# Local attention beside a long convolution on one core: projections and turning in row halves, other engines for taps, filter sums and gate, a new order

## The chip, the cores and the metric

The kernel runs on one core of a Trainium2 chip. The metric is the device time of one execution in microseconds (us). A second execution, taken with the hardware profiler, gives the profile: what each engine did and when. The core has a matrix engine (TensorE, PE in the profile; its weight loads are shown apart as PEld), VectorE (DVE), ScalarE (ACT), GpSimd (POOL), SyncE (SP, which here only starts transfers), and DMA queues. TensorE sums into PSUM, a memory of eight banks; everything else lies in the on-chip memory SBUF.

## The reference

Two independent parts, whose results stand side by side in the output (2048 rows of 1152 columns, bf16). Part A is attention over a short, dilated window; part B is a shift convolution of four taps, a product, a convolution as long as the sequence, and two more products.

```python
# part A: x is 2048 x 576, 32 heads of 18
qkv = x @ wqkv                                  # wqkv is 576 x 1728
idx = pos[:, None] - 2 * arange(8)[None, :]     # each row sees itself and 7 earlier rows, every second one
logits = einsum("bhsd,bhswd->bhsw", q, k[idx]) * 18 ** -0.5      # idx < 0: -1e9
o = einsum("bhsw,bhswd->bhsd", softmax(logits), v[idx])
a = o.reshape(1, 2048, 576) @ wo
# part B: q, k, v are 2048 x 576
kv = (sum of k shifted by t = 0..3 rows, times shift_k[:, 3 - t]) * v
y = irfft(rfft(kv, 4096) * rfft(ssm_k, 4096))[:2048] + kv * ssm_D
b = q * y
return concatenate([a, b], axis=-1)
```

## The kernel before, in words

**Storage and order.** All data lie in one SBUF tile, `mem`, at offsets worked out by hand; so nearly every row of the profile reads `mem`. PSUM is the tile `PS`: eight banks, used as four pairs. The work is a list of 675 named steps (`Op`; 745 after the change). A step may take one or two pairs of PSUM banks (a `Box`), hold them over several steps, and give them back. The string `ORDER`, a table of numbers in base 36, sets in which order the steps are emitted; a number divided by six is the step, and the remainder says which pair it takes, or, for a step that takes none and can go to either engine (`move`), that VectorE does it (remainder 1) and not ScalarE. Each engine and each DMA queue then does its own instructions in that order, and waits on semaphores for the others. So a step that waits holds up everything behind it on its engine.

**Start.** L330 (`heat`) runs 13 matmuls on zeros. `load_w` brings the projection weights, 576 columns of each of q, k and v (`comp` 0, 1, 2) in one transfer for the first four row blocks of 128 and two copies of the last 64 rows. x comes transposed by DMA (L196), except rows 512 to 1023, which come as they are and are turned on TensorE (`turn_x`, L316).

**Projections** (`project`). A unit computes one column tile `ct` (five of them: four of 128, one of 64) of one `comp` for one half `hh` of the sequence (1024 rows). The contraction runs over four row blocks of 128 (`full`, L419, matmuls on the whole array) and one of 64 (`tails`, L429: two matmuls, each on one half of the array's rows, working at the same time). The v units and the last column tile also split the array's columns in two. ScalarE copies the result out (L445; L450 for the last tile). For v, GpSimd then copies 16 edge columns between the blocks (`edges`, L402), and short DMAs do so for the last tile (`p14`, `p24`).

**Attention.** Logits: VectorE multiplies q with four shifted k at once (`l`, L473), TensorE sums the products over a head with 0/1 matrices (`L`, L481). After softmax, VectorE multiplies the weights with shifted v (`w`, L725), TensorE sums over the window (`a`, L739, two PSUM pairs), ScalarE copies the sums out (L745), and TensorE multiplies by `wo` (L790, whose result ScalarE copies out, L795).

**Convolution.** Per pair of row blocks, `taps` runs the four shifted products as diagonal matmuls into PSUM (L535), in two halves, one with its rows backwards. VectorE multiplies the result in PSUM by v (L543). `fold` turns the product: it forms a sum and a difference of the two halves while it transposes, as two matmuls of 256 columns with the joined matrices identity and plus or minus identity (`F1`, `F2`; L556, L557, and L570, L571 for the last columns). ScalarE copies the result (L561, L575). The filter gets the same treatment once (`load_filter`, `fold_filter`): a copy `ho` of its upper half is negated (`hn`), and ten accumulating DMAs from GpSimd's queue add the lower half. Then come the spectra of the filter (L581, L582, L605, L606) and of the input (L645, L660), each copied out by `move` (L188 on VectorE, L190 on ScalarE); their products on VectorE (L835, `products`), summed on TensorE (L859) and copied out (L870); the way back by L892 and L896; and the `gate`: VectorE forms the upper half and multiplies it by q (L911, L912), TensorE mirrors the lower half with the matrices that `flip` builds on GpSimd (L921), and VectorE multiplies that, out of PSUM, by q (L925).

Of the kernel before, what the change touches and what calls it, by code (L numbers as in the profile page):

```python
# [17 lines left out]
1o u 26 0 10 20 6 86 8u 1c 90 c 1u 7c 8c 6o 6u 2p 70 2c 96 2u 32 19 36 2i 1i 76 b0 66 3o bx 3u 3c 3i  # L18
a8 80 5c cp c0 40 b6 i c6 130 o 1ki ac ar ai 5i bc 4o cu 6i au 4i bi no dl bo o0 5o d0 dw nv e0 d6
oo 5u ce dc e6 oc 4c o6 ci ou 8i 46 oi po 9c i0 fk do 8o el 7i 7o fo p0 7u ew eo 1f6 136 pc rc 14c  # L20
f9 f0 4u pi fc 9w qc p6 a0 9l pu q0 9o qi i8 50 qo hl 140 qu 14v ho q6 150 ic r0 56 ii 13p r6 60 14l
13e 156 13u ri j6 ro 14o k7 13i jc 16o 146 jq ji kc ir 18c ki ju m1 hu fu k0 6c m6 mc iu 16c 15c j0
177 xo g0 kr 17u 17c l0 15i ku lp y0 l6 16x n6 xw 170 186 g6 lu yc 180 16i 161 18u gl ru ec 166 s0
17i gc s6 y6 go yi yo mi 15p lf 15u gv li z0 17o 1al 19u yu 1ao z6 zc h0 h9 sc 1fv 190 mu zo hc 1a9
1g0 zi zu 1ac 100 1g6 1hd 18i n0 19i tx 1hi 10c 19c 106 1ho 1j1 1hu 10u 1a0 mo 18o u0 110 u6 10i 196
116 si uf 19o so 1ji ui uo su t0 1i3 1jo 10o t6 tc 1i6 11c 1ik 11i ti to 1mc 1k3 1io 11o 1mi 11u uu
1iu 120 1gw v0 1mo v6 1mu 1bu 126 1fc nc 1h0 12c 12i 1j6 12o 1h6 1bk 1k6 wj 12u 1l0 1bo 1lo vx wo
1ku 1ge 1n6 1lu 1fi 1q6 w0 1fo ni 240 1n0 1gi 1oi 23f 1ou 246 w7 1go 1p0 23i wu 1oo 1nc wc vf x0 1d1
26e vi 1d6 vo 1ju 1dc 1ni 26i 1ic 1av 1di 1dq 1b0 233 1o0 1jc 2f0 1m0 1no 236 1ko 1du 1li 1qi 24e
1pc 1nu 1qc 263 1qo 24i 1cc 1pi 251 266 1e2 256 1o9 1e6 1p6 26p 1ci 25e 26u 1c0 1oc 1b7 1po 25i 25r  # L30
1c6 23q 1bc 1qu 1su 25u 1pu 1l6 23u 1lc 1so 2k0 1cq 1q0 24r 1ec 1r6 1m6 1si x6 1z1 1kc xc xi 1sc 1r0
1zi 1z6 1cu 201 1zo 1rc 1zu 1eu 1zc 20k 1f0 206 1ru 24u 1ri 20o 1ro 1t0 20u 1s2 1uf 1ui 1u0 1t6 1ej
1s6 1vo 1wl 1u6 1ww 1wo 280 1y6 1x0 27f 1tc 1eo 1w8 211 1wc 27i 1ti 27q 216 223 286 2fi 1to 27u 226
2fo 22c 1vx 1tu 20c 1ye 2fu 21c 2fc 1w0 2go 2g0 1yi 1xx 2g6 21k 1y1 2hi 2gu 21o 22l 2h0 21u 2ju 1ve
22o 2m0 2ho 1vj 1ur 22u 2hu 2k6 2ko 28e 1uu 28o 2nc 1yp 28i 1x9 1yu 28v 272 1xc 2li 2kc 276 2ki 1v3
2ku 2ge 1v6 2pu 2l0 2lo 2lu 2gi 2h9 2qc 2m6 292 2hc 2mc 29o 296 2ad 2mu 1xl 2ai 2i2 2f6 1xo 2l7 2wc
2i6 29u 2n2 2po 2qu 2n6 2mi 2ni 2q0 2mo 2j8 2no 2ic 2b3 2lc 2jc 2q6 2ro 2b6 2qi 2qo 2bc 2bl 2r0 2s0
2si 29e 2r6 2oo 29i 2cj 2ii 2bo 2ou 2nw 2co 2tc 2cu 2ru 2o0 2bu 2s6 2to 2sc 2u6 2aq 2so 2e3 2au 2su
2p0 2o6 2d1 2p6 2oc 2iw 2e6 2a0 2wu 2d6 2c3 2a6 2dc 2ti 2c6 2tu 2u0 2j0 2cc 2rf 2uc 2wi 2ji 2ek 2ri
2xc 2ui 2wo 2t3 2eo 2eu 2zi 2x0 2io 2t6 2x6 2pc 2xi 2xo 2oi 2vl 2xu 2dk 300 2zc 2do 2zo 2zu 326 306  # L40
30c 2jo 2uq 30i 32o 2uu 30o 2pi 2du 321 30u 2ec 32c 2v0 32i 32u 2vo 330 2vu 336 2v6 2y3 310 2vc 2w0
31j 2y6 33e 316 2w6 31o 2yc 31u 2yv 2yi 33i 31c 2z0 2yo 348 33o 2z6 33u 34c 340 34i
# [7 lines left out]
PAIRS = ((0, 1), (1, 2), (2, 3))  # L50


class Box:


    ps, step = None, 1024


class Op:
# [3 lines left out]
    vector = False  # L63
# [5 lines left out]
def emit(op, slot, PS):  # L69
    if op.take:  # L70
        a, b = (slot, slot + 1) if op.take == 1 else PAIRS[slot]
        op.box.ps, op.box.step = PS[:, 2 * a:2 * a + 2], 1024 * (b - a)
    Op.vector = slot == 1 and not op.take
    op.fn()
# [10 lines left out]
def kernel(  # L85
# [13 lines left out]
    nc = tc.nc  # L99
# [206 lines left out]
    def turn_x():  # L306

        dma("xn", M(OT1, [[D, 4], [1, D]]), xf[512:1024, :].rearrange("(sb p) c -> p sb c", p=128), nc.scalar)
        for u in range(3):
# [3 lines left out]
            def unit(box=box, kbs=kbs):  # L313
# [7 lines left out]
            op(f"nx{u}e", (lambda box=box, dst=dst: act(dst, box.ps, ACT.Copy)) if u < 2 else  # L321
               (lambda box=box, dst=dst: nc.vector.tensor_copy(dst, box.ps[:, 0:1, :])), box, free=True)
# [80 lines left out]

    def project(comp, ct, hh):
        o, pad = ((qat, 0), (kat, PAD), (vat, PAD))[comp]
        o = o(ct, hh)
        box = Box()
        nm = f"p{comp}{ct}{hh}"
        cols = (0,) if comp < 2 and ct < 4 else (0, 1)
        jps = (0, 1) if ct < 4 else (0,)  # L410
        tail_first = (comp == 1) if comp < 2 else ct % 2 == 1
        two = comp == 0 and hh == 0 and ct < 4

        def full(jp, first, last):
            for kb in range(4):
                ws = wcol(comp, kb, ct)
                for a in cols:
                    p = slice(64 * a, 64 * a + 64) if len(cols) > 1 else slice(0, 128)
                    mm(box.ps[p, jp, :], ws[a % len(ws)], xT(kb, 1024 * hh + 512 * (jp ^ a), 512),  # L419
# [585 lines left out]
```

## Time and profile before

| | |
|---|---|
| timed runs | 209.07, 209.44, 209.53 us (median 209.44) |
| the profiled execution's span | 207.9 us |
| time around that span, against the median | 1.54 us |
| instructions in it | 7147 |
| PE, matmuls | 3173 |
| DVE / ACT / POOL instructions | 147 / 173 / 105 |

The span is what the profiler records from the first instruction to the last. Below, "busy" is the share of the span in which an engine had an instruction running; a slice is a fortieth of the span, some 5.2 us, and its digit the busy share in tenths. A row with a time in front is from the timeline: start and length in us of a run of like instructions, engine, line, tile, and the form of the operands (`xN` counts them). A row that starts with a line number is a group of like instructions over the whole span: busy time, mean length of one in ns, and behind the second bar the engine's idle time just ahead of them and what ended it. A row from the view of waits has the engine, the waiting line, what released it, and then the sum, the number and the longest of these waits. On TensorE, matmuls of one kind overlap in the records (one of 512 columns lasts 0.39 us there, though the next starts long before), so the distance from start to start is the cost, not the length of one.

### The profile page before, as it was taken

The page shows a single profiled execution, that of the slowest core. Times are in us where ns is not written, and L with a number is a line of the kernel's source. Part 1 is how long each engine was busy: PE and PEld are TensorE (multiplying, and loading weights), DVE is VectorE, ACT ScalarE, POOL GpSimd, SP SyncE. Part 2 cuts the span into 40 slices and gives each one's busy share as a digit, 9 for nine tenths or more (in the row PEclk, how much of TensorE's full clock was granted, in tenths as well). Part 3 has the DMA queues.
Part 4 walks back from the last instruction along what each step waited for, and adds up shares of the span by engine and source line. Part 5 has one row for each costly group of instructions (what it writes and reads, how often), then busy time and mean ns, then how long its engine had stood idle before and what let it go on. Part 6 is the DMA issues. An engine that isn't in the chain of part 4 may idle for free.

```text
span 207.9 us, 7147 instructions
## 1 busy us (share of the span) xinstructions
PE 197.1 (95%) x3173; PEld 133.1 (64%) x3173; DVE 177.1 (85%) x147; ACT 142.3 (68%) x173; POOL 56.9 (27%) x105
## 2 busy tenths in 40 slices
PE   7899999999999999999998969998999999999991
PEld 2433334554644557778787857685689878787690
DVE  7306899769878898889999998999999998999963
ACT  2525479875977715578989857988898767665541
POOL 7981033001041195010899900000003020110000
PEclk9999999999999999999999999999999999999998
DMA  6998979999999959945880263106345865749834
GB/s 170 225 223 150 199 150 194 162 185 130 116 180 213 203 99 188 184 110 120 181 221 6 42 162 103 32 3 199 126 167 114 230 177 141 184 131 255 260 126 114
DMA packets 55254, 32.09 MB, mean 154 GB/s; under 512 B 42032, under 2 KB 52408, under 8 KB 55224
## 3 DMA queue, kind: packets, MB, share of 16 engines
q1 hardware_dynamic: 52520, 26.33, 57.2%
q0 software_dynamic: 2176, 4.73, 13.3%
q10 hardware_dynamic: 528, 0.59, 1.0%
q8 instruction: 24, 0.39, 0.8%
q14 instruction: 6, 0.05, 0.1%
HBM read 5.90 MB, written 4.72 MB: 51 GB/s over the span
## 4 chain that ended last, share of the span: by engine, by line
PE 84%; DMA 5%; ACT 5%; DVE 2%; SPq 1%; issue 1%; DVEq 0%
PE PS L419 24%; PE PS L790 10%; PE PS L892 7%; PE PS L859 6%; PE PS L660 5%; PE PS L481 5%; PE PS L429 4%; PE PS L535 4%; PE PS L645 3%; PE PS L739 3%; ACT mem L745 3%; DMA mem<-in_A_wqkv_dram 3%; DMA mem<-in_A_wo_dram 2%; PE PS L581 2%; PE PS L921 2%; DVE mem L725 2%
## 5 line engine op out<-in xcount | busy, mean ns | idle before, releaser
L419 PE MATMUL PS<-mem 128*64 128x512 bf16 (+1 forms) x304 | 51.5, 385 | 0.7 <-DMA mem<-in_A_wqkv_dram 0.7
L473 DVE TENSOR_TENSOR mem<-mem 128x4096 bf16<-128x4096 bf16 (+1 forms) x20 | 40.7, 2074 | 7.0 <-PE PS L481 4.2
L725 DVE TENSOR_TENSOR mem<-mem 128x4096 bf16<-128x4096 bf16 x18 | 40.3, 2290 | 1.9 <-PE PS L739 1.2
L419 PEld LDWEIGHTS <-mem 128*64 128x64 bf16 (+1 forms) x304 | 26.6, 144 | 22.1 <-issue 6.8
L835 DVE TENSOR_TENSOR mem<-mem 128x4608 bf16<-128x4608 bf16 (+3 forms) x21 | 38.4, 1867 | 1.6 <-PE PS L859 1.4
L190 ACT ACTIVATE mem<-PS 128x768 bf16<-128x768 f32 (+1 forms) x49 | 35.2, 761 | 5.8 <-PE PS L582 2.7
L445 ACT ACTIVATE mem<-PS 128x1024 bf16<-128x1024 f32 x24 | 24.2, 1022 | 19.6 <-PE PS L419 11.8
L193 POOL DMA_DIRECT2D mem<-mem x16 | 13.8, 1009 | 80.9 <-ACT mem L870 45.3
L402 POOL COPY mem<-mem 64x16 bf16<-64x16 bf16 x24 | 18.9, 788 | 22.4 <-ACT mem L445 21.6
L790 PE MATMUL PS<-mem 128*128 128x288 bf16 x160 | 21.9, 286 | 0.9 <-DMA mem<-in_A_wo_dram 0.9
L660 PE MATMUL PS<-mem 128*128 128x192 bf16 x192 | 18.7, 246 | 0.2 <-ACT mem L874 0.2
L790 PEld LDWEIGHTS <-mem 128*128 128x128 bf16 x160 | 15.3, 98 | 5.2 <-DMA mem<-in_A_wo_dram 1.2
L892 PE MATMUL PS<-mem 128*128 128x192 bf16 x192 | 17.7, 246 | 0.1
L660 PEld LDWEIGHTS <-mem 128*128 128x128 bf16 x192 | 15.9, 98 | 1.6 <-issue 1.2
L892 PEld LDWEIGHTS <-mem 128*128 128x128 bf16 x192 | 15.8, 98 | 1.2 <-issue 1.0
L859 PE MATMUL PS<-mem 32*32 32x384 bf16 x960 | 13.9, 325 | 1.3 <-ACT mem L745 0.9
L795 ACT ACTIVATE mem<-PS 128x576 bf16<-128x576 f32 x16 | 10.4, 651 | 5.4 <-PE PS L790 4.5
L543 DVE TENSOR_TENSOR mem<-PS,mem 128x512 bf16<-128x512 f32 (+1 forms) x20 | 11.5, 630 | 2.5 <-PE PS L535 2.4
L859 PEld LDWEIGHTS <-mem 32*32 32x32 bf16 x960 | 9.5, 88 | 5.0 <-issue 2.2
L896 ACT ACTIVATE mem<-PS 128x768 bf16<-128x768 f32 x12 | 9.6, 810 | 4.4 <-PE PS L892 4.4
L870 ACT ACTIVATE mem<-PS 128x1536 bf16<-128x1536 f32 x6 | 8.7, 1451 | 5.4 <-PE PS L859 5.2
L429 PE MATMUL PS<-mem 64*64 64x512 bf16 (+1 forms) x76 | 11.7, 412 | 0.0
(113 smaller groups left out, 285.7 us busy)
## 6 DMA issues: line engine op xcount, KB each, us to landing
mem<-mem SPq DMA_DIRECT2D x16, 256.0 KB, 4.2
mem<-mem POOLq DMA_DIRECT2D x8, 288.0 KB, 5.5
out_dram<-mem SPq DMA_DIRECT2D x16, 144.0 KB, 2.9
mem<-in_B_q_dram SPq DMA_DIRECT2D x4, 576.0 KB, 4.4
mem<-mem SPq DMA_DIRECT2D x6, 384.0 KB, 4.1
mem<-mem POOLq DMA_DIRECT2D x6, 384.0 KB, 4.1
mem<-in_A_wqkv_dram SPq DMA_DIRECT2D x3, 576.0 KB, 5.1
out_dram<-mem SPq DMA_DIRECT2D x6, 288.0 KB, 3.5
```

Source lines behind the costliest of these rows:

```text
L190: act(o, i, ACT.Copy, scale=scale)
L402: nc.gpsimd.tensor_copy(M1(to, PAD)[64 * a:64 * a + 64], M1(frm, PAD)[64 * a:64 * a + 64])
L419: mm(box.ps[p, jp, :], ws[a % len(ws)], xT(kb, 1024 * hh + 512 * (jp ^ a), 512), start=first and kb == 0, stop=last and kb == 3, tile_posi ...
L429: mm(box.ps[p, jp, :], ws[a % len(ws)][64 * r:64 * r + 64], xT(4, 1024 * hh + 512 * r, 512)[64 * r:64 * r + 64], start=first, stop=not fir ...
L445: op(nm + "e", lambda: act(M(o + pad, [[KH if comp == 2 else 512, 2], [1, 512]]), box.ps, ACT.Copy), box, free=True)
L473: op(f"l{hh}{ug}{ct}", lambda prod=prod, nt=nt, qo=qo, ko=ko, ug=ug: tt(M(prod, [[nt, 4], [1, nt]]), M(qo, [[0, 4], [1, nt]]), M(ko + 2 + ...
L660: mm(box.ps[:, gi // 2, TH * (gi % 2):TH * (gi % 2) + TH], M1(TX + 1024 * c + 512 * pm + 128 * gi, 128), M1(AB + 2304 * i + 1152 * c + 576 ...
L725: op(f"w{n}{ct}", lambda: tt(M(P, [[2048, 2], [256, W], [1, 256]]), M(XB[n], [[2048, 2], [256, W], [1, 256]]), M(vo + 2, [[256, 2], [2, W] ...
L790: mm(box.ps[:, h, 0:HD], M1(lhs, 128), M1(rhs, HD), start=(i == 0), stop=(i == 4))
L835: tt(M(pr + 768 * k, [[2304, n], [768, m], [1, 768]]), M(BS + i * SPB + o + PL * k, [[SPB, n], [PL, m], [1, 768]]), M(VS + (3 - j + i) * S ...
L859: mm(view(box.ps[32 * c:32 * c + 32], box.step * (r // 2) + 512 * (r % 2), [[TH, 2], [1, TH]]), I32S[w][32 * r:32 * r + 32], M(pr + src + ...
L892: mm(box.ps[:, pm, TH * c:TH * c + TH], M1(TI + 512 * sl + 256 * pm + 128 * c, 128), M1((YT if j else YRS[0]) + 1536 * t + 768 * pm + TH * ...
```

## The change

It has five parts.

**Projections.** All units but q of the first half of the sequence are now two steps, `q` and the plain one, and each of their matmuls uses one half of the array's rows, 64 (`quadrants`, L415). In the first step, bank 0 is summed by the lower rows and bank 1 by the upper rows at the same time; in the second the other way round. Both steps add into the same PSUM banks, so the second must not begin before the first has ended: a no-op (`between`, steps with `n` at the end of their name) on another engine waits for the last matmul of the first step, and the first matmul of the second waits for the no-op. The engine is chosen by the step's remainder in `ORDER`. The last column tile of 64 columns shares a unit between q and k (`p40`, `p41`) and between both halves of the sequence for v (`p24`). The weights of q and k come in two transfers, columns 0 to 255 and the rest.

**Turning.** `fold` uses matmuls of 128 columns on 64 rows, two beside each other, one on each half of the rows (L598), where it had matmuls of 256 columns on all rows. The copy out of each is two copies now, of which `move` lets each go to ScalarE or VectorE.

**Taps.** ScalarE copies the tap sums out of PSUM as bf16 (L584), and VectorE multiplies them by v in SBUF (L585).

**Filter sums.** VectorE forms the difference and the sum of the filter's halves (L660, L661) in place of the negation and the accumulating DMAs; the edge row of the filter is handled by one DMA and a copy on ScalarE (L667).

**Gate.** For the first three row blocks ScalarE copies the mirrored half out of PSUM (L970), and one VectorE product (L976) replaces two out of PSUM. The last block stays as it was.

**Order.** `ORDER` is a new table throughout. Its core as a diff (the tables are left out):

```diff
     def load_w(comp, eng):
         b = WW + 5 * D * comp
-        dma(f"w{comp}", M(b, [[D, 4], [1, D]]),
-            A_wqkv[0:512, comp * D:(comp + 1) * D].rearrange("(kb p) a -> p kb a", p=128), eng)
+        for c0, c1 in ((0, 256), (256, D)) if comp < 2 else ((0, D),):
+            dma(f"w{comp}" + "b" * (c0 > 0), M(b + c0, [[D, 4], [1, c1 - c0]]),
+                A_wqkv[0:512, comp * D + c0:comp * D + c1].rearrange("(kb p) a -> p kb a", p=128), eng)
...
+    def phase(box, ph, runs):
+        first = None
+        for n in range(max(len(run) for run in runs)):
+            for run in runs:
+                if n < len(run):
+                    o, w, i, pos = run[n]
+                    ins = mm(o, w, i, start=ph == 0 and n == 0, stop=ph == 1 and n == len(run) - 1, tile_position=pos)
+                    first = first or ins
+        if ph:
+            tc.add_manual_dep(first.ins, box.half.ins.name, AFTER, reason="the other half of the rows sums here too")
+        box.half = ins
+    def between(nm, box):
+        def fence():
+            nop = (nc.gpsimd, nc.vector, nc.scalar, nc.sync)[Op.slot].nop()
+            tc.add_manual_dep(nop.ins, box.half.ins.name, AFTER, reason="behind the first halves")
+            box.half = nop
+        op(nm + "n", fence, box)
+    def quadrants(box, ph, parts):
+        runs = []
+        for lo, cols, r1, x0, bank, tail in parts:
+            r = r1 ^ ph
+            h = slice(64 * r, 64 * r + 64)
+            runs.append([])
+            for kb in [0, 1, 2, 3] + [4] * (tail == r):
+                w = cols(kb)
+                m = w.ap[-1][1]
+                runs[-1].append((box.ps[lo:lo + m, bank, :], w[h], xT(kb, x0, 512)[h], (64 * r, lo)))
+        phase(box, ph, sorted(runs, key=lambda run: run[0][3]))
...
...
     def taps(pr):
-                op(f"t{pr}{n}{'hl'[lo]}", lambda box=box, s=s, b=b, lo=lo, n=n, nb=nb: tt(
-                    M(KV + 1024 * n + 256 * lo, [[512, nb], [1, 256]]), view(box.ps, b, s), M(VT + 1024 * n + b, s),
-                    ALU.mult), box, free=bool(lo))
+                op(nm, lambda box=box, s=s, b=b, kv=kv: act(kv, view(box.ps, b, s), ACT.Copy), box, free=bool(lo))
+                op(nm + "m", lambda s=s, b=b, n=n, kv=kv: tt(kv, kv, M(VT + 1024 * n + b, s), ALU.mult))
...
     def fold(pr):
+        def turn(box, h, b, mt, to):
+            k = slice(64 * h, 64 * h + 64)
+            o = view(box.ps, 512 * h + to, [[256, 2], [1, 64]])
+            return [(o, w[k], M(ID + i + 64 * h, [[128, 2], [1, 64]])[k], i == 128, h)
+                    for w, i in ((M1(b + 128 * mt, 128), 128), (M1(b + 256 + 128 * mt, 128), 0))]
+        def both(todo):
+            for pair in zip(*todo):
+                for o, w, i, first, h in pair:
+                    mm(o, w, i, start=first, stop=not first, tile_position=(64 * h, 0))
...
-                        o = box.ps[:, n // 2, 256 * (n % 2):256 * (n % 2) + 256]
-                        b = KV + 1024 * n + 512 * ab + 128 * mt
-                        mm(o, M1(b, 128), F1, start=True, stop=False)
-                        mm(o, M1(b + 256, 128), F2, start=False, stop=True)
+                        both([turn(box, h, KV + 1024 * n + 512 * ab, mt, 64 * n) for h in range(2)])
...
     def load_filter(d):
-        op(f"hn{d}", lambda: move(M1(HO + 2 * D * d, 2 * D), M1(HU + 2 * D * d, 2 * D), -1.0))
+        op(f"ho{d}", lambda: tt(o, f, h, ALU.subtract))
+        op(f"he{d}", lambda: tt(h, h, f, ALU.add))
...
-        op(f"hz{b}", lambda: nc.gpsimd.memset(o0, 0.0))
-        for d in (2 * b, 2 * b + 1):
-            for t, nm in ((HU, "e"), (HO, "o")):
-                dma(f"h{nm}{d}", M1(t + 2 * D * d, 2 * D), M1(FT + 2 * D * d, 2 * D), nc.gpsimd, accum_op=ALU.add)
+        op(f"hz{b}", lambda: act(o0, f0, ACT.Copy))
...
     def gate(j, c0, n):
+            if n == D:
+                op(f"{nm}e{e // w}", lambda box=box, e=e: act(M(y + e, [[D, 2], [1, w]]), box.ps[:, :, 0:w], ACT.Copy), box,
+                   free=True)
...
+        if n == D:
+            op(nm + "l", lambda: tt(M(qb, d), M(y, d), M(qb, d), ALU.mult))
```

The new table moves instructions on every engine. Three places follow.

On TensorE, where the first turning begins, before (L605 and L606 are the last matmuls of a filter spectrum, L556 and L557 the first of `fold`):

```order
L605 LDWEIGHTS mem
L605 MATMUL PS<-mem 128x288
L606 LDWEIGHTS mem
L606 MATMUL PS<-mem 128x288
L556 LDWEIGHTS mem
L556 MATMUL PS<-mem 128x256 [waits DVE_49]
L557 LDWEIGHTS mem
L557 MATMUL PS<-mem 128x256
```

And the same turning now (L520 is the summing of logits, L598 the turning in row halves, L415 a v projection):

```order
L520 LDWEIGHTS mem
L520 MATMUL PS<-mem 32x512
L598 LDWEIGHTS mem
L598 MATMUL PS<-mem 128x2x64 [waits Activation_49]
...
L598 LDWEIGHTS mem
L598 MATMUL PS<-mem 128x2x64
L415 LDWEIGHTS mem
L415 MATMUL PS<-mem 64x512 [waits Activation_49]
```

The turning has moved from behind the filter's spectra to between the logits' sums and the projections of v, and a unit is 16 matmuls of 128 columns where it was 8 of 256.

On TensorE, at the end of the first k projections, before (L419 the full matmuls, L429 the tails):

```order
L419 LDWEIGHTS mem
L419 MATMUL PS<-mem 128x512
L429 LDWEIGHTS mem [waits DMAHW5_49]
L429 MATMUL PS<-mem 128x512 [waits DMAHW2_49]
L429 LDWEIGHTS mem [waits DMAHW1_49]
L429 MATMUL PS<-mem 128x512 [waits DVE_49]
```

And at one of the new units, with the wait for the no-op on SyncE between its halves (`p110`; the rows between stand for seven more matmuls of the second half):

```order
L415 LDWEIGHTS mem
L415 MATMUL PS<-mem 128x512
L415 LDWEIGHTS mem [waits SP_sequencer_49]
L415 MATMUL PS<-mem 128x512
...
L415 LDWEIGHTS mem [waits DMAHW1_49]
L415 MATMUL PS<-mem 128x512 [waits Activation_49]
```

The change of division within a unit is gone, and a wait for another engine's sequencer has come in front of the second half; 22 such rows stand on TensorE.

On GpSimd, the end of its queue before (L402 the edge copies of v, L245 and L246 the matrices of `flip`, L193 transfers: first the filter's accumulating ones, at the end six that add one row block's sums to the next):

```order
L193 DMA mem<-mem 1x2x576
L193 DMA mem<-mem 128x1152
L402 COPY mem<-mem 64x16 x22
L245 MEMSET mem 128x128
L246 AFFINE_SELECT mem<-mem 128x128
L245 MEMSET mem 128x128
L246 AFFINE_SELECT mem<-mem 128x128
L193 DMA mem<-mem 128x1536 x6
```

And now (L406 the edge copies, L249 and L250 `flip`):

```order
L406 COPY mem<-mem 64x16 x20
L249 MEMSET mem 128x128
L250 AFFINE_SELECT mem<-mem 128x128
L249 MEMSET mem 128x128
L250 AFFINE_SELECT mem<-mem 128x128
L406 COPY mem<-mem 64x16 x4
L197 DMA mem<-mem 128x1536 x6
```

The accumulating DMAs ahead of the edge copies are gone, and `flip` stands ahead of the last four edge copies.

More of the change, by code (lines that the diff above doesn't have):

```diff
@@ L23 @@
[L23 to L27, printed above, removed]
@@ L72, in emit @@
         op.box.ps, op.box.step = PS[:, 2 * a:2 * a + 2], 1024 * (b - a)
-    Op.vector = slot == 1 and not op.take
+    Op.vector, Op.slot = slot == 1 and not op.take, slot
     op.fn()
@@ L404, in project @@
     def project(comp, ct, hh):
-        o, pad = ((qat, 0), (kat, PAD), (vat, PAD))[comp]
-        o = o(ct, hh)
+        o = (qat, kat, vat)[comp](ct, hh)
         box = Box()
         nm = f"p{comp}{ct}{hh}"
[L409 to L419, printed above, removed]
-                       start=first and kb == 0, stop=last and kb == 3, tile_position=(0, 64 * a))
@@ L441, in project @@
[L441 to L454 removed]
+        t0 = 1024 * hh
@@ L567, in unit @@
             for mt in range(2):
[L568 to L571 removed]
+                both([turn(box, h, KV + 4096, mt, 64 * mt) for h in range(2)])
         op(f"f{pr}2", unit, box, 1)
```

161 lines of the change are left out of this document (90 added, 71 removed).

## The prediction

> **What bounds the kernel now.** I read the page first: its span, the busy shares, the slices and the chain that ended last.
>
> ```profile
> span 207.9 us, 7147 instructions
> PE 197.1 (95%) x3173; PEld 133.1 (64%) x3173; DVE 177.1 (85%) x147; ACT 142.3 (68%) x173; POOL 56.9 (27%) x105
> ...
> PE   7899999999999999999998969998999999999991
> ...
> DVE  7306899769878898889999998999999998999963
> ...
> PEclk9999999999999999999999999999999999999998
> ...
> PE 84%; DMA 5%; ACT 5%; DVE 2%; SPq 1%; issue 1%; DVEq 0%
> ```
>
> TensorE is busy 95% of the span at its full clock and carries 84% of the chain. VectorE is not far behind, at nines from slice 19 on. So the time is TensorE's queue, with VectorE as the next limit. A busy TensorE hides short stalls, since the ends of matmuls are modelled; I therefore read its pace from start to start, and its stalls from its own view of waits:
>
> ```profile
> PE PS L330 <- DVE pib L207: 1.3, 1, 1.3
> PE PS L581 <- ACT mem L745: 1.1, 2, 0.6
> PE PS L859 <- ACT mem L745: 0.9, 1, 0.9
> PE PS L790 <- DMA mem<-in_A_wo_dram: 0.9, 1, 0.9
> PE PS L570 <- ACT mem L745: 0.8, 1, 0.8
> PE PS L419 <- DMA mem<-in_A_wqkv_dram: 0.7, 1, 0.7
> PE PS L921 <- ACT mem L896: 0.6, 1, 0.6
> ```
>
> Beside the start, only some 4.3 us are waits: 2.8 for ScalarE's copy of the attention sums (L745, which holds two of the four PSUM pairs), 0.9 for the output weights, 0.6 at the end. The rest is a full queue: a microsecond of matmul work that goes is nearly a microsecond, as long as VectorE keeps up.
>
> The sum below is made against the profiled execution (207.9 us). The timed runs have a median of 209.44, so 1.54 us lie around the span; I add them at the end.
>
> **1. Turning the convolution input (`fold`).**
>
> ```profile
> 52.52 0.27 PE L556 MATMUL PS<-mem 128*128 128x256 bf16 x1
> ...
> 55.03 0.27 PE L557 MATMUL PS<-mem 128*128 128x256 bf16 x1
> 55.13 0.29 PE L605 MATMUL PS<-mem 128*128 128x288 bf16 x1
> ...
> 38.22 0.62 PE L375 MATMUL PS<-mem 128*32 128x128 bf16 x32
> 38.67 0.60 PE L481 MATMUL PS<-mem 128*32 128x512 bf16 x8
> ```
>
> From 52.52 to 55.13 stand 24 of these matmuls: 109 ns each. L556, L557, L570 and L571 make 72 in all, 7.8 us. After the change 144 matmuls of 128 columns run in pairs, one on each half of the array's rows. A step of 128 columns takes 56 ns (L375: 32 matmuls, four at a time, so 8 steps from 38.22 to 38.67). That is 72 x 56 = 4.0 us: **-3.8**. If the halves followed each other it would be 144 x 56 = 8.1, a loss of 0.3; a gain above 3.9 (half of 7.8) is excluded, since each pair still streams half the columns. I take -3.8, because row halves already run side by side here, as the next rows show.
>
> **2. Projections in row halves.**
>
> ```profile
> 12.51 0.39 PE L429 MATMUL PS<-mem 64*128 64x512 bf16 x2
> 12.83 1.04 PE L419 MATMUL PS<-mem 128*128 128x512 bf16 x4
> ...
> 15.63 2.76 PE L419 MATMUL PS<-mem 128*128 128x512 bf16 x12
> 18.33 0.61 PE L429 MATMUL PS<-mem 64*128 64x512 bf16 x4
> 18.87 1.90 PE L419 MATMUL PS<-mem 128*128 128x512 bf16 x8
> ```
>
> Twelve full matmuls take 2.70 us up to the next start, so 216 ns each and 0.1 more; four half-height ones take 0.54, which is two steps of 216 and 0.1 again. So a pair of row halves costs as much as one full matmul, and each change of the array's division costs 0.1 us (two matmuls from 12.51 to 12.83: one step and 0.1). A unit of two row blocks stays at nine steps (before 8 full and one pair, after 5 and 4 pairs), which gains nothing by itself. The last column tile was 5 steps in each of six units and is now 9 in each of three: 3 x 0.216 = -0.65. Along TensorE's instructions the division changed 100 times and changes 86 times now: -1.4. Together **-2.05**, from 0 (if the half-height steps lose what the divisions gain) to -2.5.
>
> **3. The new wait between halves.** Each of 23 units stops until a no-op on another engine (12 on GpSimd, 9 on ScalarE, one each on SyncE and VectorE) has seen the first half end; everything behind it on TensorE stops too. A half-height matmul lasts 0.39 us (row at 12.51), and in 22 of 23 units at least four steps of other work (4 x 0.216 = 0.86) stand in between, so the no-op has about half a microsecond. One unit (`p210`) has nothing between and loses some 0.3. The no-op can be late when its own engine is: behind GpSimd's constants and edge copies, or behind a ScalarE eviction. Ends: 0, and 23 x 0.39 = 9.0. I take **+0.5**, near the lower end, since the cover stands in the order itself.
>
> **4. VectorE and ScalarE.**
>
> ```profile
> L543 DVE TENSOR_TENSOR mem<-PS,mem 128x512 bf16<-128x512 f32 x16 | 10.2, 683 | 2.4 <-PE PS L535 2.4
> L501 DVE TENSOR_TENSOR mem<-mem 128x512 bf16<-128x512 bf16 x2 | 0.8, 422 | 0.0
> L911 DVE TENSOR_TENSOR mem<-mem 128x1152 bf16<-128x1152 bf16 x3 | 2.3, 751 | 0.0
> L925 DVE TENSOR_TENSOR mem<-PS,mem 128x576 bf16<-128x576 f32 x6 | 4.5, 754 | 1.2 <-PE PS L921 1.0 <-ACT mem L896 0.2
> L188 DVE TENSOR_SCALAR mem<-PS 128x768 bf16<-128x768 f32 x3 | 2.9, 956 | 0.5 <-PE PS L645 0.5
> ...
> L450 ACT ACTIVATE mem<-PS 128x512 bf16<-128x512 f32 x6 | 3.6, 597 | 3.1 <-PE PS L419 1.6 <-PE PS L429 1.5
> ...
> 20.00:40.00 20.00, 20.00 (x208) 8.19 (x210) 17.69 (x12) 14.71 (x17) 3.60 (x5) 1.00 1.06 179
> ```
>
> VectorE: 16 tap products fall from 683 to 422 ns (-4.2; the four small ones with them -0.5; a reversed bf16 product is not in the trace, at 683 this gain is nothing), 8 filter sums come (+6.0), six gate products of 754 become three of 751 (-2.3), and it takes over some evictions (one of 768 columns and four others, about +3.5 at 956 ns each or less). Sum +2.5, to 179.6. ScalarE: 16 tap copies of 597 and four small ones (+11), six gate copies (+4), less four negations and the larger fold copies; about +11, to 153 of some 200 us. Neither is on the path as long as VectorE's idle time shrinks: it has 30.8 us of it, and in 20.00:40.00 it stands 2.3 us while TensorE is full. So I cost it at **0** here and as rival C below. The ten accumulating DMAs that go had no waiter on TensorE: no gain.
>
> **5. What the order moves.**
>
> ```profile
> 5.08 1.46 PE L316 MATMUL PS<-mem 128*128 128x128 bf16 x20
> ...
> 8.09 0.39 PE L419 MATMUL PS<-mem 128*128 128x512 bf16 x1 [0.68 <-DMA mem<-in_A_wqkv_dram]
> ...
> 99.12 15.59 POOL L402 COPY mem<-mem 64x16 bf16<-64x16 bf16 x14 [1.90 <-ACT mem L445]
> ```
>
> The start: projections began at 8.09, held 0.68 by the first third of the weights. Only 256 of its columns are needed now, but all 13 heating matmuls stand ahead of the turned x, whose copy the first projection needs: about 8.5, **+0.4** (-0.7 to +1.5). The output weights: before, two of their loads stood in SyncE's queue behind copies that wait for the second attention pass; now all stand ahead of them: **-0.9**. Attention copies: the next units in the order still ask for the held PSUM pair after each pass, but later; I keep 2.0 of 2.8: **-0.8**. GpSimd: its 16-element edge copies crawl beside VectorE's products (14 in 15.6 us); `flip` now stands ahead of the last four, which the second half's products need: **+0.3** (0 to 2).
>
> Sum: -3.8 -2.05 +0.5 +0 +0.4 -0.9 -0.8 +0.3 = -6.35, so a span of 201.55 and a time of **203.1 us**.
>
> **Rivals.**
>
> A. The halves' weight loads set the pace of the turns.
>
> ```profile
> L556 PEld LDWEIGHTS <-mem 128*128 128x128 bf16 x32 | 3.1, 98 | 0.4
> L316 PEld LDWEIGHTS <-mem 128*128 128x128 bf16 x20 | 1.3, 107 | 0.7 <-DMA mem<-in_A_x_dram 0.7
> ```
>
> If a pair cannot go faster than one load of 98 ns, the turns take 72 x 98 = 7.1 us and gain 0.7 instead of 3.8: **206.2**. For it: every turn needs its own load. Against it: L316's 20 loads of 107 ns are done in 1.3 us, one per 65 ns, so loads overlap. The Trainium skill, "TensorE: Matmul & The Clock Gate", section "LDWEIGHTS (loading the stationary operand)", speaks against this change: a load takes its columns / 1.2 ns, and "a 32×128 weight load takes the same time as a 128×128 weight load". By it (an estimate) 144 loads one by one are 144 x 107 = 15.4 us, 11.4 more than my 4.0, and the time 214.5. The trace agrees with its duration and not with such a queue.
>
> B. The other side: the no-ops come late. Where the no-op's engine is behind, TensorE loses the whole 0.39 us in each unit: +9.0 instead of +0.5, **211.6**. It decides from (209.4 - 203.1 + 0.5) / 23 = 0.3 us a unit. Against it: the cover of 0.86 us.
>
> C. VectorE becomes the bound.
>
> ```profile
> 0.00:20.00 20.00, 18.05 (x91) 7.29 (x92) 8.15 (x15) 8.45 (x9) 14.21 (x54) 1.00 0.87 196
> ```
>
> These windows hold the busy time of TensorE, its weight loads, VectorE, ScalarE and GpSimd in turn. From 20 us on VectorE was busy 177.1 - 8.2 = 168.9 of 187.9 us, so idle 19.0. With 2.5 more work in a span of 201.55 its idle must fall to 10.1. If it falls half as far, to 14.6, the span is 206.0 and the time **207.5**. For it: VectorE's products wait for ScalarE's copies, of which there are more. Against it: its waits in the rows of part 4 are for TensorE, which comes earlier.
>
> D. More goes than I count: with attention starting earlier, the 2.0 us kept for PSUM go and the start stays at 8.1: 203.1 - 2.4 = **200.7**.
>
> E. It does not do what it says: the divisions and turns gain, and the new order loses as much elsewhere: 209.4.
>
> **How the numbers follow.** Forecast 203.1: 0.50; D 0.19; C 0.12; A 0.08; E 0.04; B 0.07. Forecast, D, C and A are faster by over 0.2% (about what a measurement of this kernel can tell from no change): 0.89, less 0.02 for a worse C; E is the same, 0.05; slower 0.08. The range takes in D with about a microsecond to spare, and C: 199.8 to 207.6, and leaves out B and E.
>
> **What would show it.**
>
> ```profile
> 105.97 2.00 PE L739 MATMUL PS<-mem 32*32 32x512 bf16 x128
> ```
>
> The first attention sums start here before the change; they should start about 4.5 us earlier. The turns' lines at about 56 ns a pair (A: 98). No wait of TensorE on a sequencer's no-op above a microsecond in all (B). VectorE's idle time after 20 us near 10 (C: 14 or more). No wait for the output weights. The forecast is wrong if TensorE's waits grow by more than 3 us, which only the interplay of four queues in the new order can bring.

## The result, and the profile after

The changed kernel takes **206.67 us** (median of 5 runs, 205.25 to 207.37) against 209.44 before: a ratio of 0.9865, 95% interval 0.9831 to 0.9898. Two later series of five runs of the same kernel gave 205.60 (ratio 0.9806, 0.9782 to 0.9830) and 205.74 (0.9824, 0.9800 to 0.9848). It is faster, as forecast, but by 2.8 to 3.9 us and not by 6.3; the time lies inside the range. The profiled execution is the fastest of the first five (205.25 us).

The page of the kernel after, its span, busy times, slices and chain:

```profile
span 203.6 us, 7863 instructions
PE 192.0 (94%) x3517; PEld 131.7 (65%) x3517; DVE 178.1 (88%) x156; ACT 148.3 (73%) x201; POOL 47.9 (24%) x93
...
PE   7799999999999999999989899989999999999971
...
DVE  4646989899998899998999999999798989979833
...
PE 90%; ACT 5%; issue 2%; DVE 1%; DVEq 0%; ACTq 0%
```

TensorE still sets the time. What is new is "issue" at 2% of the chain (1% before): time in which the engine waited for nothing that the profile shows. The view of TensorE's waits says where:

```profile
PE PS L903 <- issue: 1.9, 2, 1.5
PE PS L334 <- DVE pib L211: 1.3, 1, 1.3
PE PS L451 <- ACT mem L194: 1.1, 1, 1.1
PE PS L703 <- ACT mem L789: 0.6, 1, 0.6
PE PS L965 <- ACT mem L940: 0.6, 1, 0.6
PE PS L598 <- ACT mem L789: 0.5, 1, 0.5
...
PE PS L834 <- issue: 0.2, 1, 0.2
```

The waits for the output weights (0.9 before) are gone, those for the attention copies (L789 now, L745 before) have halved. But the largest wait beyond the start has no releaser: L903, the summing of the products. The timeline shows it in the middle of one unit (start, length, line, count, idle time ahead):

```profile
191.87 1.11 PE L903 MATMUL PS<-mem 32*32 32x384 bf16 x73
194.49 0.90 PE L903 MATMUL PS<-mem 32*32 32x384 bf16 x55 [1.51 <-issue]
```

These 128 matmuls are four steps in a row (Z320 to Z323), and the 73rd and the 74th lie inside one of them (Z322), with no wait of any kind between them. The 73rd started at 192.65; the 74th started 1.83 us later than the pace of these matmuls would have it. In this text a "stop" is such a delay beyond the engine's own pace.

**What stops there: the instructions themselves.** The page counts a DMA queue of kind "instruction" (packets, MB, share of 16 engines), after, and before:

```profile
q8 instruction: 27, 0.44, 0.9%
```

```profile
q8 instruction: 24, 0.39, 0.8%
```

Each of its packets is 16 KB (0.44 MB by 27). The trace holds 7050 instructions of TensorE after (a load and a matmul for each product, and 16 steps of its sequencer) and 6364 before, and fewer than 300 of any other engine; 27 and 24 packets for these fit blocks of 256. Counted along the trace, the 74th matmul is instruction 6850, which is 194 + 26 x 256; its weight load, one instruction earlier, ran at 192.65. The other four stops in the last 50 us begin at 194 plus a multiple of 256 as well. The DMA packets of that queue, beside the starts of the blocks, for some of the last blocks of the changed kernel (us):

```
block first   it    next block's fetch   next block  after the   stop
instruction  starts  starts    ends      starts      fetch
4802         150.66  152.23   153.12     154.66       1.55       0.30
5570         167.75  171.41   172.34     173.75       1.42       0.40
5826         173.75  177.22   178.19     179.40       1.21       0.72
6082         179.40  181.66   182.62     184.08       1.46       0.33
6338         184.08  185.76   186.83     190.25       3.42       0
6594         190.25  192.21   193.09     194.49       1.40       1.83
```

In these rows a fetch starts 1.6 to 3.7 us after the block ahead of it has begun and lasts about 1 us. Where TensorE stops, the next block begins 1.2 to 1.6 us after the fetch has ended; no block of any traced run begins sooner than that. Where the 256 instructions of a block are done before, TensorE stops. In the last row the fetch starts 2.0 us into a block of the short 32-row sums: at 190.3 to 192.2 the data queue filled the DMA engines, and the packet came in the window behind. The DMA view of the two windows, 190.3 to 192.2 and 192.1 to 193.2:

```profile
q1 hardware_dynamic: 661, 0.73, 107.0%
...
q1 hardware_dynamic: 102, 0.09, 24.8%
q8 instruction: 1, 0.02, 5.0%
```

The five stops make 3.6 us. (The view of waits puts the one at 154.66 down to ScalarE, whose copy ended 0.29 us before; in the runs below the distance to that copy varies from 0.15 to 0.44, and that to the end of the fetch from 1.3 to 1.6.) Before, there was one, at instruction 5826 (0.67 us); the timeline shows it as a break of the same kind:

```profile
191.53 1.11 PE L859 MATMUL PS<-mem 32*32 32x384 bf16 x73
192.98 0.90 PE L859 MATMUL PS<-mem 32*32 32x384 bf16 x55 [0.34 <-issue]
```

The Trainium skill, "Runtime: NRT & Kernel Launch", section "Instruction fetch mechanics", says that an engine's instructions come in 16 KiB blocks of 256 through its own DMA queue, and that crossing such a boundary is mostly hidden. The trace agrees with the block. Of the 26 boundaries in the changed kernel 21 show no stop, so most are hidden here too; the other five cost 3.6 of 203.6 us.

**Where the time went.** TensorE's span divided by kind of work: from a step's first matmul to the next step's, so that a wait counts to the step ahead of it, worked out from the starts of all matmuls (us).

```
                                         before   after   change   forecast
projections, turning, taps                77.21   71.18    -6.03     -5.35
wait for the output weights                1.07    0       -1.07     -0.9
spectra and way back (copies' waits)      53.04   51.13    -1.91     -0.8
start (heating, turned x)                  6.83    7.04    +0.21     +0.4
logits, attention sums, gate, filter      28.79   29.49    +0.70     +0.3
product sums and output projections       35.76   39.58    +3.82      0
sum                                      202.70  198.42    -4.28     -6.35
```

The terms that were forecast came to -8.1 us, 1.75 more than forecast. The growth of the last row was not forecast. All five stops lie in it, and their growth makes 2.9 of it (3.58 - 0.67); the other 0.9 are waits at the ends of its steps, the largest 0.4 and 0.3 for ScalarE's copies (L918, L839).

### The profile page after: what moved, and what is told of

Read it like the earlier page. It is cut to its first block, busy times and chain, and to the rows that moved or that the text cites. A ratio compares the mean times of both kernels' runs of the same rounds, so it can differ in the third digit from the quotient of the medians.

```text
span 203.6 us, 7863 instructions
## 1 busy us (share of the span) xinstructions
PE 192.0 (94%) x3517; PEld 131.7 (65%) x3517; DVE 178.1 (88%) x156; ACT 148.3 (73%) x201; POOL 47.9 (24%) x93
## 4 chain that ended last, share of the span: by engine, by line
PE 90%; ACT 5%; issue 2%; DVE 1%; DVEq 0%; ACTq 0%
PE PS L415 23%; PE PS L834 9%; PE PS L936 8%; PE PS L703 7%; PE PS L903 7%; PE PS L520 5%; PE PS L574 4%; PE PS L783 4%; PE PS L451 4%; PE PS L688 3%; ACT mem L789 3%; PE PS L598 2%; PE PS L334 2%; PE PS L628 2%; PE PS L965 2%
## 5 line engine op out<-in xcount | busy, mean ns | idle before, releaser
L415 PE MATMUL PS<-mem 64*64 64x512 bf16 (+1 forms) x612 | 51.3, 383 | 0.2
L194 ACT ACTIVATE mem<-PS 128x768 bf16<-128x768 f32 (+3 forms) x63 | 42.3, 728 | 8.9 <-PE PS L321 4.4
L415 PEld LDWEIGHTS <-mem 64*64 64x64 bf16 (+1 forms) x612 | 29.1, 146 | 18.6 <-issue 2.9
L406 POOL COPY mem<-mem 64x16 bf16<-64x16 bf16 x24 | 22.1, 920 | 39.2 <-PE PS L415 34.4
L197 POOL DMA_DIRECT2D mem<-mem x6 | 5.2, 874 | 61.3 <-ACT mem L914 43.4
L936 PE MATMUL PS<-mem 128*128 128x192 bf16 x192 | 17.5, 246 | 0.2 <-ACT mem L914 0.2
L903 PE MATMUL PS<-mem 32*32 32x384 bf16 x960 | 14.7, 326 | 2.2 <-issue 1.9
L936 PEld LDWEIGHTS <-mem 128*128 128x128 bf16 x192 | 16.0, 98 | 0.7 <-ACT mem L914 0.4
L839 ACT ACTIVATE mem<-PS 128x576 bf16<-128x576 f32 x16 | 10.2, 656 | 6.0 <-PE PS L834 5.5
L903 PEld LDWEIGHTS <-mem 32*32 32x32 bf16 x960 | 9.3, 88 | 6.9 <-issue 5.5
L192 DVE TENSOR_SCALAR mem<-PS 128x768 bf16<-128x768 f32 (+3 forms) x8 | 7.2, 904 | 4.4 <-PE PS L321 2.1
L520 PE MATMUL PS<-mem 128*32 128x512 bf16 x160 | 11.0, 382 | 0.0
```

What stands on the lines that cost most here:

```text
L194: act(o, i, ACT.Copy, scale=scale)
L406: nc.gpsimd.tensor_copy(M1(to, PAD)[64 * a:64 * a + 64], M1(frm, PAD)[64 * a:64 * a + 64])
L415: ins = mm(o, w, i, start=ph == 0 and n == 0, stop=ph == 1 and n == len(run) - 1, tile_position=pos)
L520: mm(boxes[ug].ps[32 * j:32 * j + 32, uu, :], E, M(prod + 2 * uu * nt + 256 * jo, [[nt, 2], [1, 256]]), start=(ct == 0), stop=(ct == 4), t ...
L903: mm(view(box.ps[32 * c:32 * c + 32], box.step * (r // 2) + 512 * (r % 2), [[TH, 2], [1, TH]]), I32S[w][32 * r:32 * r + 32], M(pr + src + ...
L936: mm(box.ps[:, pm, TH * c:TH * c + TH], M1(TI + 512 * sl + 256 * pm + 128 * c, 128), M1((YT if j else YRS[0]) + 1536 * t + 768 * pm + TH * ...
```

## The experiments

The two theories in the expectations: **instruction theory**, the lost time is TensorE waiting for blocks of its instructions; **VectorE theory** (rival C of the prediction), VectorE's products end too late in the last 30 us.

**e1, e12: the changed kernel again.**

> The changed kernel, nothing altered, to see what its runs differ by (205.25 to 207.37 us before, and the profile shown is of the fastest). Instruction theory: TensorE stops where a block of 256 of its instructions has not arrived; in the profile shown these stops (no releaser, at instructions 5826, 6082, 6338 and 6850 of its queue) make 3.3 us, before the change 0.7 us. A trace of a slower run (206.5 to 207.4) then has more of such stops, 4 to 5 us, at the same distance of 256 instructions, and all other waits as before within 0.5 us. VectorE theory (the products in the last 30 us end too late): the further time lies in waits for VectorE or ScalarE.

> The changed kernel, nothing altered, beside the run with late stores on the same chip: 205.3 to 207, with 3 to 4 us of stops without a releaser in its trace.

Measured 205.60 and 205.74 us, the profiled spans 203.9 and 204.0. The stops sum to about 3.3 and 3.0 us, at instructions 5058, 6082, 6338 and 6850 in both; ahead of 5826 stands a wait for a transfer instead (L936, 0.4 and 0.7). The four longer executions of the first series (206.5 to 207.4) were not traced, and what they had more of stays open.

**e2, e5: without the stores of the attention's rows.** The 16 stores are left out in the changed kernel and in the one before; that half of the output is not written.

```diff
-        dma(nm + "s", outf[r0:r0 + 128, 0:D], st)
+        op(nm + "s", lambda: None)
```

> The 16 stores of the attention's output rows are left out (that half of the output is not written); nothing in the kernel waits for them but ScalarE's reuse of three store buffers. Instruction theory: the fetches of the last 40 us start sooner after the block before them has begun (up to 3.5 us now), the stops without a releaser fall from 3.3 to about 1 us, and the time to about 204 us (203.3 to 205). VectorE theory: no transfer is on the path, the time stays at 206.7 within 0.4.

> The kernel before without the 16 stores of the attention's output rows (that half is not written). Instruction theory: the stores cost time only through late blocks of instructions, and before the change there was one such stop of 0.67 us: 208.8 us (208.6 to 209.5). Rival, the stores cost the same 2.4 us in any kernel (their transfers delay others that the path waits for): 207.1.

Changed kernel: 203.21 us (ratio 0.9689, 0.9664 to 0.9715), just below the range expected by the instruction theory; span 200.8. The stops fall from 3.6 to 0.7 us, that in Z322 from 1.83 to 0.51; its timeline:

```profile
190.43 1.12 PE L903 MATMUL PS<-mem 32*32 32x384 bf16 x74
191.73 0.89 PE L903 MATMUL PS<-mem 32*32 32x384 bf16 x54 [0.18 <-issue]
```

The fetch for this block now starts 0.2 us after the block ahead of it has begun, not 2.0. The kernel before does not get faster at all without its stores: 210.10 us (ratio 1.0031, 1.0005 to 1.0057), span 208.0, its one stop 0.57 instead of 0.67. That is far from the rival's 207.1, and 0.6 above the instruction theory's range too; where these 0.6 come from is open. So the stores cost time in the changed kernel and not in the one before; the changed kernel's span falls by 2.8 us without them, about as much as its stops (2.9). The VectorE theory falls: VectorE's work is the same in both runs of the changed kernel. Its windows from 20 us on, of the changed kernel and then without stores (TensorE, loads, VectorE, ScalarE, GpSimd):

```profile
20.00:203.60 183.60, 174.41 (x3398) 123.75 (x3392) 166.91 (x139) 138.89 (x191) 36.73 (x44) 1.00 0.61 142
```

```profile
20.00:200.80 180.80, 173.70 (x3395) 124.20 (x3392) 166.86 (x139) 138.88 (x191) 36.97 (x44) 1.00 0.59 131
```

VectorE does 166.9 us of work in both, and the second span is 2.8 us shorter: VectorE had idle time to give.

**e3, e4: the blocks moved along the program.** 64 matmuls of one column stand in place of four heating matmuls.

```diff
-            for _ in range(n):
+            for _ in range(64 if nm == "hot1" else 0):
+                mm(box.ps[0:32, 1, 0:1], M1(PR, 32)[0:32], M1(PR, 1)[0:32], start=True, stop=True, tile_position=(0, 0))
+            for _ in range(0 if nm == "hot1" else n):
```

> Four of the 13 heating matmuls are replaced by 64 matmuls of one column, all ahead of the first projection: 120 more instructions in TensorE's queue, so that each block of 256 ends 120 instructions earlier in the program. Instruction theory: the stops without a releaser in the last 40 us move to other instructions (those at 5706 + 256 n in the old count) and their sum changes from 3.3 us to something between 0.5 and 4.5; the time follows by the same amount, beside what the start loses. VectorE theory: they stay at the same matmuls with the same length, the time changes by the start alone (0 to +0.7).

> The same 64 matmuls in place of four heating ones in the kernel before. Instruction theory: its one such stop (0.67 us, at instruction 5826) moves or goes and others may come: 208.5 to 211.5 us. VectorE theory: 209.4 to 210.2, the start alone.

Changed kernel: 208.76 us (ratio 0.9966, 0.9938 to 0.9994). The start lost 1.8 us, more than expected. The stop in the product sums moved by 60 matmuls, which is 120 instructions, to the edge of the same counted block:

```profile
193.12 0.37 PE L905 MATMUL PS<-mem 32*32 32x384 bf16 x13
195.46 1.94 PE L905 MATMUL PS<-mem 32*32 32x384 bf16 x115 [1.96 <-issue]
```

In the changed kernel 73 matmuls ran ahead of the break, and now 13: it follows the count of instructions and not the work. The sum of the stops stayed (3.25 us), so the time tells little here and the place everything. The span is 3.3 us longer than the changed kernel's: 1.8 at the start, 0.5 in a wait for a transfer (L630), and some 1.3 behind the long break, where the granted clock was 0.5 from 196.5 to 199.9 us (matmuls of 192 columns stand 160 ns apart there, and 81 ns behind it). The row of the granted clock in slices of 5.2 us:

```profile
PEclk9999999999999999999999999999999999999969
```

Whether the stop brings that on is not shown: in the changed kernel the clock stayed full behind a stop of 1.83 us.

The kernel before: 213.08 us (ratio 1.0184, 1.0145 to 1.0223), outside both expectations. The profiled execution took 211.7 us (span 210.0), and what the median has more stays open; in it the start lost 0.5, a wait for a transfer 0.4, and the stops grew from 0.67 to 2.18, one of them in the way back, which no VectorE product feeds directly:

```profile
194.68 1.16 PE L894 MATMUL PS<-mem 128*128 128x192 bf16 x12
196.99 1.81 PE L894 MATMUL PS<-mem 128*128 128x192 bf16 x20 [1.15 <-issue]
```

**e6: the old turning in the changed kernel (without stores).** `fold` uses the 72 matmuls of 256 columns on all rows.

```diff
-                        both([turn(box, h, KV + 1024 * n + 512 * ab, mt, 64 * n) for h in range(2)])
+                        o = box.ps[:, n // 2, 256 * (n % 2):256 * (n % 2) + 256]
+                        b = KV + 1024 * n + 512 * ab + 128 * mt
+                        mm(o, M1(b, 128), F1, start=True, stop=False)
+                        mm(o, M1(b + 256, 128), F2, start=False, stop=True)
```

> The kernel of the second experiment (changed, no attention stores, 203.21 us) with the turning by 72 matmuls of 256 columns on all rows, as before the change; the copies stay two. By the prediction's first term: 3.8 us more, less five divisions of the array that it saves (0.5): 206.6 (206.0 to 207.2). Rival, weight loads set the pace of the halves: 0.7 more, 203.9. Rival, VectorE is the limit and hides TensorE's work: 0 to 1.5 more, up to 204.7.

Measured 207.86 us, above the range expected, 4.65 more than e2; the span 204.9, 4.1 more (the rest lies around the span). Of these 4.1, 0.4 stand at the start and 0.2 in stops, which leaves 3.5. The prediction's first term holds, both rivals fall. The changed kernel's timeline shows the pace itself:

```profile
62.75 0.62 PE L598 MATMUL PS<-mem 64*128 64x128 bf16 x16
63.30 1.36 PE L415 MATMUL PS<-mem 64*64 64x512 bf16 x20
```

16 matmuls up to the next start in 0.55 us: eight pairs of 56 ns and one division of 0.1. The loads of 94 ns that rival A feared set no pace.

**e7: projections on all rows in the changed kernel (without stores).** The same two steps a unit, by banks and not by row halves, and no no-ops.

```diff
-            op(nm + "q", lambda: quadrants(box, 0, parts), box, 1)
-            between(nm, box)
-            op(nm, lambda: quadrants(box, 1, parts), box)
+            op(nm + "q", lambda: full_rows(box, 0, parts), box, 1)
+            op(nm + "n", lambda: None)
+            op(nm, lambda: full_rows(box, 1, parts), box)
```

> The kernel of the second experiment (203.21 us) with the projections on all rows of the array in the same two steps (one bank, then the other and the tails), without the no-ops between; the shared last tiles stay shared. The division of the array then changes 128 times, not 86. By the prediction's second and third terms: 42 x 0.1 = 4.2 more, less 0.5 for the waits that go: 206.9 (206.3 to 207.4). Rival, half-height steps cost what the divisions save: 203.2 within 0.5. Rival, the no-ops are late (0.39 us in each of 23 units): faster, below 202.

Measured 209.75 us, 6.5 more than e2 where 3.7 was expected. 0.9 of it is the start, some 0.4 are stops (one of 1.1 us), which leaves 5 to 6. Some 2 us come between 80 and 95 us, where the v units stand: one of these lasts 1.5 us on all rows (L452 and its tails, L461, up to the next unit), where four steps and one of 216 ns and two divisions make 1.3.

```profile
86.43 1.14 PE L452 MATMUL PS<-mem 128*64 128x512 bf16 x8
87.50 0.49 PE L461 MATMUL PS<-mem 64*64 64x512 bf16 x4
87.92 1.14 PE L452 MATMUL PS<-mem 128*64 128x512 bf16 x8
```

The loads of v's columns last 179 ns there, against 97 for whole tiles; that such a load does not hide behind a change of the division would account for the rest, but is only argued.

**e8, e11: the last three attention stores later.** o1101, o1110 and o1111 are stored behind the last sums; a change of `ORDER` alone, here SyncE's queue:

```diff
+L197 DMA out_dram<-mem 128x2x576 x3
+L197 DMA mem<-in_B_q_dram 128x4x576 x2
 L197 DMA out_dram<-mem 128x2x576
-L197 DMA out_dram<-mem 128x576
-L197 DMA out_dram<-mem 128x2x576 x2
-L197 DMA out_dram<-mem 128x576
-L197 DMA mem<-in_B_q_dram 128x4x576 x2
-L197 DMA out_dram<-mem 128x576
-L197 DMA out_dram<-mem 128x2x576
+L197 DMA out_dram<-mem 128x576 x3
```

> The changed kernel with the last three attention stores (o1101, o1110, o1111) behind the last sums (Z323) on SyncE's queue. Instruction theory: the fetch that ends at 193 us in the profile meets less traffic, the stop of 1.8 us at instruction 6850 shrinks to about 0.7, and the time falls by 0.5 to 1.2 us, unless the late stores set the end (then up to 1 us slower). VectorE theory: no change (within 0.3), or slower by the late stores.

> The changed kernel with its last three attention stores behind the last sums, again, beside the changed kernel on the same chip: 0.5 to 1.2 us faster than that by the instruction theory (its profile gave 202.5 against 203.6 and 203.9), equal by the rival.

Measured 204.98 and 204.48 us. The second ran beside e12 (205.74), and its ratio to the kernel before (0.9761, 0.9737 to 0.9786) lies clear of e12's (0.9800 to 0.9848). The 128 matmuls of the last sums run through, their stop is 0.2 us:

```profile
192.28 1.89 PE L903 MATMUL PS<-mem 32*32 32x384 bf16 x128
```

So this kernel is faster than the one before and than the changed one.

**e9, e10: the new turning alone in the kernel before**, and the same with 56 more matmuls of one column, which bring the added instructions to 256.

```diff
+                        both([turn(box, h, KV + 1024 * n + 512 * ab, mt, 64 * n) for h in range(2)])
...
+            for _ in range(56 if nm == "o0000" else 0):
+                mm(box.ps[0:32, 0, 0:1], EHS[0][0:32], EHS[0][0:32, 0:1], start=True, stop=True, tile_position=(0, 0))
```

> The kernel before with the change's turning alone (144 matmuls of 128 columns in pairs; two ScalarE copies where one was): 144 more instructions in TensorE's queue, all ahead of 122 us. By the prediction's first term alone: 3.8 us less, and seven more divisions of the array (0.7 more): 206.3 (205.9 to 206.6). Instruction theory: the same gain until the first product sums (Z000, 143.2 us before, 140.1 then), but the blocks of 256 end 144 instructions earlier in the program, and the stops without a releaser grow from 0.7 to 2 to 3 us: 207.6 to 208.8. Rival, the turn is paced by weight loads: 209.4 or more.

> The same, with 56 more matmuls of one column ahead of the first output projection (o0000, where TensorE waits 1.07 us for the output weights in the profile before): 112 more instructions, so 256 more than before in all, and the blocks end at the same instructions of the program as before from there on. Instruction theory: the stops fall back to 0.6 to 0.9 us; the 56 matmuls take 1.6 us of which the wait hides 1.0: 206.2 to 207.2, faster than the kernel with the new turning alone by 0.8 to 2 us although it does more. Rival (the position of the blocks does not matter): slower than that kernel by 0.6 us.

e9: **212.25 us, slower than before** (ratio 1.0106, 1.0072 to 1.0139), though TensorE has less to do, and above the 207.6 to 208.8 that the instruction theory expected. The rival's number (209.4 or more) came, but not its mechanism: 16 pairs take 1.00 us, which is 56 ns each and a change of the division, and not 98 each:

```profile
93.60 1.07 PE L558 MATMUL PS<-mem 64*128 64x128 bf16 x32
94.60 0.71 PE L419 MATMUL PS<-mem 128*64 128x512 bf16 x4
```

From 95 us up to the last sums the kernel was 0.8 to 1.3 us ahead of the one before, not 3.2; two waits behind the turning are new, 0.4 for ScalarE's copy and 0.5 for a load of the filter. Then come two stops of 1.5 and 2.7 us, together 4.2:

```profile
197.25 1.30 PE L865 MATMUL PS<-mem 32*32 32x384 bf16 x92
200.89 0.71 PE L865 MATMUL PS<-mem 32*32 32x384 bf16 x36 [2.34 <-issue]
```

Here the fetch started 4.7 us after the block ahead of it had begun. e10: 209.79 us, 2.5 less than e9 with more work; the stops in the last 50 us are 0.47 in all. It is no faster than the kernel before (ratio 0.9981 to 1.0021), above what was expected: by 115 us it was 1.0 and not 3.2 us ahead, with a new stop of 0.6 at instruction 2242, in the attention sums, and the 56 matmuls cost 0.3 beyond the wait that hides them. That the place of the blocks decides 2 us and more is shown; the sizes expected were off.

## Why the prediction was wrong

- **The step that failed** stands in its first part: "a microsecond of matmul work that goes is nearly a microsecond, as long as VectorE keeps up". It priced a matmul by its columns alone, and 344 more of them at nothing. TensorE must also be given its instructions: in the profile after the change it stopped 3.6 us for late blocks of them, against 0.67 before. Moving the blocks moved the stops (e3, e10), and without the stores that delayed the fetches the same kernel takes 203.21, close to the forecast's 203.1. Part of that agreement is chance: the forecast terms brought 1.75 more than forecast, small waits of 0.9 took some of it back, and stops of 0.7 stay.
- **The missed sign was in view.** The row of TensorE's waits "L859 <- issue" of 0.3 in the profile before (its break in the timeline is shown above) had no releaser, and the prediction left it aside:

```profile
PE PS L859 <- issue: 0.3, 1, 0.3
```

- **Turning:** -3.8 forecast; 56 ns a pair as forecast, 3.5 us by e6. Right. Rival A did not come.
- **Row halves:** right in kind, mis-sized. With turning and taps, the work on the array fell by 6.03 instead of 5.35 (the table above). The turning's own steps make 3.25 of it in the new order, which leaves 2.8 for the projections and taps with their new wait, where 1.55 was forecast (2.05 - 0.5). e7 puts the row halves at 5 to 6 us in the new order, where the division would change 128 times otherwise, not 100.
- **The wait between halves:** +0.5 forecast, 0.34 measured along the trace: 0.29 in `p210`, the unit without cover, as forecast, and nothing above 0.05 in any other. Rival B did not come.
- **VectorE:** work and sizes were right. The tap products last 413 ns (422 assumed), the filter sums 737 and 753, the gate 752; its sum is 178.1 (179.6 forecast). By groups:

```profile
L585 DVE TENSOR_TENSOR mem<-mem 128x512 bf16<-128x512 bf16 x16 | 6.0, 413 | 0.0
...
L660 DVE TENSOR_TENSOR mem<-mem 128x1152 bf16<-128x1152 bf16 x4 | 2.9, 737 | 0.0
L661 DVE TENSOR_TENSOR mem<-mem 128x1152 bf16<-128x1152 bf16 x4 | 2.9, 753 | 0.0
...
L976 DVE TENSOR_TENSOR mem<-mem 128x1152 bf16<-128x1152 bf16 x3 | 2.3, 752 | 0.0
```

  Its idle time after 20 us is 16.7 us where 10.1 was forecast, which the prediction had named as the sign of rival C. The sign misled. 4.5 of the difference is less work after 20 us than assumed (166.9 against 171.4), and 2.05 is the longer span. Without the stores the same work fits into 2.8 us less (e2), so VectorE was not the limit.
- **Order:** the start +0.2 (+0.4 forecast); the output weights -1.1 (-0.9); the waits for the attention copies fell by 1.5 (0.8 forecast); `flip` ahead of the edge copies cost nothing that VectorE's waits show (0.3 forecast). The first attention sums start at 99.91, 6.1 us earlier (4.5 forecast):

```profile
99.91 2.05 PE L783 MATMUL PS<-mem 32*32 32x512 bf16 x128
```

## What to carry to other kernels

A split that doubles the number of matmuls at equal columns is not free: count instructions beside columns. A break in TensorE's timeline with no releaser, inside one step, was a late block of 256 instructions here wherever it was followed up; count the instructions ahead of it. The five blocks of the changed kernel that ran out would have taken 2.4 to 5.6 us without the stop; the shortest work is that of the 32-row sums. Before a change is judged, look whether such breaks grew: here the turning that is worth 3.5 us in the new order became, made alone in the old one, a loss of 2.8, with 4.2 us of them. Transfers that nobody waits for (stores) were not free beside such a piece: moving three of them was worth 1.3 us.

## What the runs showed of the hardware that was not expected

- TensorE's stops without a releaser begin at instruction 194 + 256 n of its trace, whatever the program has there: so in eight different instruction streams, to within the few records that some traces lack. In all 14 traces no block begins less than 1.2 us after its 16 KB fetch has ended, and where TensorE stops it is 1.2 to 1.6 us.
- The fetch of a block starts between 2.6 us before and 4.7 us after the start of the block ahead of it, so only about one block is fetched in advance. For one block (the one in which the last sums stopped) the other transfers decide: 0.2 us without the stores or with three of them later, 1.7 to 2.1 with them. What sets the other distances is open: in the 4.7 us of e9 the data queue took 74.2% of the DMA engines (194 to 198.5 us), and not all of them.
- The count of instructions ahead of a piece of work changes its time: 112 more of them made a kernel 2.5 us faster (e9 to e10), and 120 more cost the kernel before 1.5 us in stops (e4).
